# Attention and long convolution on one core: the last product of VectorE's exponential made by GpSimd

## The chip, the cores and the metric

One core of a Trainium2 chip. The metric is the device time of one execution in microseconds (us). The engines are TensorE (PE in the profile; PEld its weight loads), VectorE (DVE), ScalarE (ACT), GpSimd (POOL) and SyncE (SP). GpSimd and SyncE also issue DMA transfers, each from a queue of its own that is worked off in order.

## The reference

Two independent blocks share the program, and their results stand side by side in the output:

```python
def _A_ref(x, wqkv, wo):              # x: 1 x 2048 x 512, 32 heads of 16
    qkv = ((x @ wqkv).reshape(B, S, 3, H, Dh)).transpose(2, 0, 3, 1, 4)
    scores = einsum("bhqd,bhkd->bhqk", q, k) * (Dh ** -0.5)
    p = softmax(scores, axis=-1)
    o = einsum("bhqk,bhkd->bhqd", p, v)
    return o.transpose(0, 2, 1, 3).reshape(B, S, D) @ wo

def _B_ref(q, k, v, shift_k, ssm_k, ssm_D):   # each 1 x 2048 x 512
    kv = shifted_sum(k, shift_k) * v          # 4 taps
    y = causal convolution of kv with ssm_k over 2048 positions, by FFT
    return q * (y + kv * ssm_D)
```

All inputs and the output are bf16. Part A needs 32 x 2048 x 2048 exponentials, and they are most of the work.

## The kernel before, in words

**Blocks.** A block is the scores of one head for 128 keys and 512 queries: one PSUM bank of 128x512 fp32. There are 32 groups (a set of four heads and 512 queries each), 64 blocks to a group, 2048 in all. TensorE makes the scores (`qk_mm`, L810), four heads at once in four row groups of the array.

**Two engines make exponentials.** ScalarE takes two or three blocks at a time (`emit_exp`, L835) from two sets of three PSUM banks and writes them to the ring PT. VectorE takes single blocks (`exp_on_dve`), which TensorE puts into bank BGB or the third bank of a set. [...] L902 reads the scores from PSUM, adds a constant, clips, and stores 16 bits to PTD. The other steps work from SBUF to SBUF on a pair of blocks, 128x1024 elements, in the buffers `low` and `top` of the ring RST: L910 takes the mantissa bits, L914 makes a line of them (fp16), L917 multiplies line and mantissa (the "square"), L920 takes the exponent bits into `low`, and L923 multiplies the square by the number itself into `top` (the "cube", the last product). The block's value is the sum of three terms, PTD, `low` and `top`, and the sum is made by TensorE: the matmul with V (`emit_pv`, L989) accumulates three matmuls for a VectorE block and one for a ScalarE block.

**Order.** The whole program is planned in Python when it is built. Each engine is an `Eng` with a clock `t`; `op(fn, deps, us=...)` appends an instruction, its semaphore waits and its planned end. Each step T of the main loop emits scores and ScalarE's exponentials for some chunk, the matmuls with V of earlier chunks, and background work. Queued VectorE steps stand in `flow`; `pick` and `advance` issue them where the plan says that they can start. `dve_block` decides when VectorE gets a block. In the last stretch of a group it refuses by a fixed number of remaining blocks (GAP). A VectorE pair may begin when the pair three earlier (`R_RST`) has left the ring RST. What is planned becomes a fixed instruction order on each engine; at run time only the semaphores decide.

**Part B.** The convolution is done by TensorE as matmuls of rows of the kernel (WR, streamed by SyncE's queue, L355) with KV (L1215). Results are copied to YB (L1231) and turned back by `conv_turn`: eight matmuls with a permuted identity as the moving operand (L1244), read from IDN with a step of 32 elements; then L1251 multiplies by q in QN. After the eighth turn of a half, QN is stored by GpSimd's queue and reloaded for the second half by `load_qn`, whose first transfer waits for the store. The products kv are made by L573 out of four staged quarters of v; the first three are staged in buffers that are used later for something else, and the fourth in VS2.

**GpSimd before.** It fills constants at the start (L448 to L461), builds a diagonal by an affine select on 128x2048 elements (L629), and otherwise issues DMAs (L355): 120 small ones that spread q into QT, in 15 groups of eight, 15 stores of the attention output, and the loads and stores of QN.

Further line numbers of the trace: L553 moves q out of PSUM, L562 keys, L586 values, L1060 to L1080 end a group (transposes, reciprocal, product), L1142 moves the output rows. After the change the lines have moved: L922, L926, L929 and L932 are what L910, L914, L917 and L920 were, L933 the last product, L914 what L902 was, L819 and L1000 what L810 and L989 were, L844 what L835 was, L1257 the turn.

Of the kernel before, what the change touches and what calls it, by code (L numbers as in the profile page):

```python
# [13 lines left out]
S = 2048  # L14
# [56 lines left out]
MOST_OP = 3  # L71
OVER_OP = 0.1
R_PTD = 5
R_RST = 3
EVEN = 0.85
MOST_D = 3
MORE = 0.1
# [11 lines left out]
MOST = 3  # L89
Q_DUE = 20  # L90
LOOK = 6
GAP = 7
TAIL_GAP = 0
AHEAD = 5
KZ_LATE = 8.0
# [164 lines left out]
def bass_concat_heads__mha_block__ssm_conv_h3__prompt_kernel(  # L260
# [25 lines left out]
    def sb(name, shape, dt=BF16):  # L286
        return enter(nc.sbuf_tensor(name, shape, dt))
# [19 lines left out]
    DTN = sb("DTN", [128, 2, QB])  # L307
    DR = sb("DR", [128, 2, 16], FP32)
    OUTA = sb("OUTA", [128, R_A, D])
    VS2 = sb("VS2", [128, NB * 128])  # L310
    YB = sb("YB", [128, 2, 512])
    IDN = sb("IDN", [128, 128])
    SHK = sb("SHK", [128, 4, 4])
    PTD = sb("PTD", [128, R_PTD, 2, QB])
    RST = sb("RST", [128, R_RST, 2, 2, QB])
# [4 lines left out]
    WV = WKV[:, 0:4 * D].rearrange("p (c f) -> p c f", c=4)  # L320
    WO = WKV[:, 4 * D:8 * D].rearrange("p (o f) -> p o f", o=4)
    VST = [x.rearrange("p (t d) -> p t d", t=NB)
           for x in (WR[:, R_W - 2, 0:S], WR[:, R_W - 1, 0:S], OUTA[:, :, :].rearrange("p r d -> p (r d)"), VS2[:, :])]
# [102 lines left out]
    for c in range(4):  # L426
        for x in range(2):
            src = bass.AP(tensor=v2.tensor, offset=v2[S // 2 * x + 64 * (NB - 1), 128 * c].offset, ap=[[D, 64], [-64 * D, NB], [1, 128]])
            h = dma(sp, d_kv[3 + c], VST[c][x:128:2, :, :], src, kb=256)
        h_vn.append(h)  # L430

    src = bass.AP(tensor=k2.tensor, offset=k2[0:1, 0:1].offset, ap=[[D, S // 2], [S // 2 * D, 2], [1, D]])
    dma(sp, d_kp, kt_ap[LEFT:LEFT + S, :], src, kb=2048)
    dma(sp, d_kp, kt_ap[1:LEFT:2, :], k2[S // 2 - LEFT // 2:S // 2, :], kb=8)
# [14 lines left out]
    for par in range(2):  # L449
# [4 lines left out]
    h_id0 = pool.op(lambda e: e.memset(IDN[:, :], 0.0))  # L454
    h_idn = pool.op(lambda e: e.affine_select(out=IDN[:, :], in_=IDN[:, :], compare_op=ALU.not_equal, fill=1.0,
                                              base=0, pattern=[[-1, 128]], channel_multiplier=1), [h_id0])
    pool.op(lambda e: e.memset(VA[:, :, :, 0:8 * VW].rearrange("p s k (h e) -> p (s k) h e", e=VW)[:, :, :, DH:VW], 1.0))
    h_va1 = pool.op(lambda e: e.memset(VA[:, :, :, 8 * VW:VROW].rearrange("p s k e -> p (s k) e"), 1.0))
    h_kv0 = pool.op(lambda e: e.memset(KV[:, :, NB:2 * NB, :].rearrange("p q w g -> p q (w g)").bitcast(U32), 0), us=(4.4, 4.5))
# [25 lines left out]
    def ready(u):  # L485
        if u[0] == "q":
            return (u[1] < R_Q or 2 * (u[1] - R_Q) + 1 in qk_done) and (u[1] < 2 or 2 * u[1] - 1 in h_q and at(h_q[2 * u[1] - 1]) <= pe.t + 0.5)
        if u[0] == "k":
            return u[1] < 2 or LAST[u[1] - 2] in qk_done
        if u[0] == "v":  # L490
            return u[1] < 2 or LAST[u[1] - 2] in pv_done
        if u[0] == "op":
            return (PAIRS.index((3, u[1])) if u[1] < NQB - 1 else (15, u[2] + 1)) in h_otn and h_wop[0] is not None
        return KT_OF[u[1]][0] in h_kt

    def pe_unit(u, bank, parts=(0, 1, 2, 3)):
        kind = u[0]
# [50 lines left out]
    def evac_unit(u, bank, h):  # L548
        kind = u[0]
        if kind == "q":  # L550
            p = u[1]
            last = [qk_done[2 * (p - R_Q) + i] for i in range(2)] if p >= R_Q else []
            hh = urgent(lambda e: e.tensor_scalar(QS[:, :], PS[:, bank, :], QSCALE, None, ALU.mult),  # L553
                        [h] + [h_q[2 * (p - 1) + i] if p > 1 else None for i in range(2)], us=V512)
            for par in range(2):
                for r0 in range(16 * par, 128, 32):
                    h_q[2 * p + par] = dma(pool, d_qs[p % 2][par], QT[r0:r0 + 16, p % R_Q, par, :], QS[r0:r0 + 16, :],
                                           [hh, h_qt0] + last, kb=16)
        elif kind == "k":
            _, o, sc = u  # L560
            c0 = KEYS0 if (o, sc) == (0, 0) else 0
            hh = urgent(lambda e: e.tensor_copy(KTo[:, o % 2, sc * 512 + c0:(sc + 1) * 512], PS[:, bank, c0:512]),  # L562
                        [h, qk_done[LAST[o - 2]] if o > 1 else None], us=(0.335, 0.46) if c0 else V512)
            h_k[(o, sc)] = hh
            if (o, sc) == (3, 3):
                load_wop(h)
        elif kind == "kv":
            _, c, i = u
            u0 = NB - 4 - 4 * i
            val = VST[c][:, u0:u0 + 4, :].rearrange("p b (q g) -> p b q g", g=4)  # L570
            src = PS[:, bank, :].rearrange("p (b q g) -> p b q g", b=4, g=4)
            dst = KV[:, 32 * c:32 * c + 32, u0:u0 + 4, :].rearrange("p q w g -> p w q g")
            hh = urgent(lambda e: e.tensor_tensor(dst, src, val, ALU.mult), [h, h_vn[c]], us=V512)  # L573
# [132 lines left out]
    def blk(i):  # L706
        return i // (4 * KT), (i // 4) % KT, i % 4
# [11 lines left out]
    def sub(i):  # L719
        n, k, s = blk(i)  # L720
        return n, k // 4 if n == NL else 0
# [173 lines left out]
    def exp_on_dve(b, bank, h):  # L895
# [18 lines left out]
            st["d"] = dve.op(lambda e: e.tensor_scalar(top[:, w].bitcast(FP16), low[:, w], T1, T0, ALU.mult, ALU.add), [st["d"]], us=us)  # L914

        def square(us):
            st["d"] = dve.op(lambda e: e.tensor_tensor(top[:, w].bitcast(FP16), low[:, w], top[:, w].bitcast(FP16), ALU.mult), [st["d"]], us=us)  # L917

        def power(us):
            dve.op(lambda e: e.tensor_scalar(low[:, w].bitcast(U16), lin[:, w].bitcast(U16), 0xFF80, None, ALU.bitwise_and), [st["d"]], us=us)  # L920

        def cube(us):  # L922
            st["d"] = dve.op(lambda e: e.tensor_tensor(top[:, w], top[:, w].bitcast(FP16), lin[:, w], ALU.mult), [st["d"]], us=us)  # L923
# [7 lines left out]
        st["f"][:] = [("p", dep, f, us[n], gate) for f, us, gate in ((mant, FOUR, begin), (line, FOUR, lambda: True), (square, TWO, lambda: True),  # L931
                                                                     (power, FOUR, lambda: True), (cube, TWO, lambda: True))]  # L932

    h_otn = {}
    h_mul = {}
# [236 lines left out]
    def feed_wr(k, h=None):  # L1172
# [6 lines left out]
                wr_next[0] = qd + 1  # L1179
        del wr_todo[:k]  # L1180

    def release():
        h = (pe.sem, pe.n)
        words = BLOCK - pe.at_word % BLOCK
        ends = pe.t + words / (70.0 if busy_conv() else 33.0) + SPAN - LOADED
        while wr_todo and max(dma_t[0], max(at(h) + 0.13, sp.t) + 2.95) + 528 / WR_KB - 0.85 <= ends and pe.t >= pe.crossed + 0.6:
            feed_wr(1, h)
# [46 lines left out]
            state["turn"], state["b"] = True, b  # L1234

    def conv_turn(b, bank):
        own, next_ = [bass.AP(tensor=IDN[:, :].tensor, offset=IDN[0:1, 31:32].offset, ap=[IDN[:, :].ap[0], [-1, n], [32, 4]]) for n in (32, 31)]

        def fn(e):
            ins = None  # L1240
            for k in range(4):
                for part in range(2):
                    y = YB[:, k // 2, 256 * (k % 2) + 128 * part:256 * (k % 2) + 128 * part + 128]
                    ins = e.matmul(PS[:, bank, 128 * k + 4 * part:128 * k + 128], lhsT=y, rhs=(own, next_)[part], start=part == 0, stop=part == 1)  # L1244
            return ins
        h = pe.op(fn, [bank_free[bank], h_ybw[0], h_idn], run=0.445, kind="F")
        h_yb[0] = h
        sl = b // 8
        yv = PS[:, bank, :].rearrange("p (k b g) -> p k b g", k=4, g=4)
# [3 lines left out]
        if b % 8 == 7:  # L1253
# [295 lines left out]
```

## Time and profile before

| what | value |
| --- | --- |
| median of 3 runs | 818.05 us (813.47 to 823.0) |
| the profiled execution | 816.27 us, span 814.5 us |
| ScalarE busy | 777.7 us (95%) |
| VectorE busy | 741.5 us (91%) |
| TensorE busy | 730.1 us (90%), granted clock 0.987 |
| GpSimd busy | 89.9 us (11%) |
| blocks by VectorE / by ScalarE (instruction counts) | 345 / 1703 |

The span goes from the first instruction to the last of the profiled execution; the execution's own time is a little longer. A row of groups reads: line, engine, operation, output <- input, shapes, count | busy us, mean ns of one | idle us of the engine just before them, and who ended it. Busy time counts overlapping instructions once, so a mean duration times a count is more than the busy time. A timeline row reads: start, us, engine, line, operation; several instructions in a row are merged, with their count. A row of waits reads: who waited, for whom, us in total, times, longest. A row of windows gives a stretch, its length, the busy us of PE, PEld, DVE, ACT and POOL, granted clock, DMA share and GB/s.

### The profile page before, as it was taken

How to read it: one execution, taken by the hardware profiler on the slowest of the kernel's cores; microseconds unless marked ns; L12 is line 12 of the kernel's file. 1: busy time of each engine (PE TensorE's matmuls, PEld its weight loads, DVE VectorE, ACT ScalarE, POOL GpSimd, SP SyncE). 2: the span in 40 equal slices, each digit the busy share in tenths (PEclk: the TensorE clock that was granted, in tenths of full speed). 3: DMA queues.
4: the chain of work that ended last, by engine and by line, in shares of the span. 5: the costliest groups of instructions: out<-in, count | busy, mean ns of one | idle time of the engine just before them, and what ended most of it. 6: DMA issues, size and time to landing. Idle time of an engine off the chain costs nothing.

```text
span 814.5 us, 24480 instructions
## 1 busy us (share of the span) xinstructions
PE 730.1 (90%) x10724; PEld 302.5 (37%) x10757; DVE 741.5 (91%) x1480; ACT 777.7 (95%) x633; POOL 89.9 (11%) x160
## 2 busy tenths in 40 slices
PE   7899898989889989999889988989998989898987
PEld 3333343434344333333333333333433423333344
DVE  5799999899989899989999999899999998989985
ACT  7998999999989899999999999999999998999997
POOL 4200230110010102001002400101003020000100
PEclk9999999999989999999999999999999999999999
DMA  9995056577457656677704777586774755664200
GB/s 248 250 282 188 8 125 216 198 252 254 179 184 257 216 215 233 243 271 296 266 2 147 210 277 285 181 327 228 244 274 159 236 207 207 240 234 142 53 2 28
DMA packets 83041, 164.15 MB, mean 202 GB/s; under 512 B 41232, under 2 KB 47256, under 8 KB 82680
## 3 DMA queue, kind: packets, MB, share of 16 engines
q1 hardware_dynamic: 75880, 153.61, 55.3%
q0 software_dynamic: 5856, 8.66, 4.0%
q8 instruction: 85, 1.39, 0.7%
q10 hardware_dynamic: 1200, 0.33, 0.2%
q14 instruction: 20, 0.16, 0.1%
HBM read 149.17 MB, written 8.54 MB: 194 GB/s over the span
## 4 chain that ended last, share of the span: by engine, by line
ACT 49%; DVE 30%; PE 19%; issue 1%
ACT PT L835 49%; DVE PTD L902 9%; PE PS L989 6%; PE PS L810 5%; DVE RST L917 4%; PE PS L1244 4%; DVE RST L923 3%; DVE RST L910 3%; DVE RST L914 3%; DVE RST L920 2%; PE PS L1215 1%; DVE YB L1231 1%; DVE DT L1060 1%; DVE QN L1251 1%; PE PS L526 1%
## 5 line engine op out<-in xcount | busy, mean ns | idle before, releaser
L835 ACT ACTIVATE PT<-PS 128x1536 bf16<-128x1536 f32 (+1 forms) x627 | 774.8, 1386 | 27.8 <-PE PS L810 26.4
L810 PE MATMUL PS<-QT,KTo 32*128 32x512 bf16 (+2 forms) x2248 | 249.8, 368 | 57.8 <-ACT PT L835 23.8
L902 DVE TENSOR_SCALAR PTD<-PS 128x512 uint16<-128x512 f32 x345 | 234.9, 682 | 9.9 <-PE PS L810 9.3
L989 PE MATMUL PS<-PT,VA 128*32 128x512 bf16 (+2 forms) x1873 | 184.1, 372 | 9.4 <-DVE DT L1060 5.0
L810 PEld LDWEIGHTS PS<-QT,KTo 32*128 32x128 bf16 x2248 | 66.8, 91 | 239.3 <-ACT PT L835 154.8
L1413 PE MATMUL PS<-IDN,ZW 128*32 128x512 bf16 (+3 forms) x549 | 126.3, 325 | 0.1
L355 POOL DMA_DIRECT2D QT<-QS x120 | 61.3, 519 | 536.3 <-DVE QS L553 534.1
L917 DVE TENSOR_TENSOR RST<-RST 128x1024 f16<-128x1024 bf16 (+1 forms) x174 | 117.6, 679 | 2.3
L923 DVE TENSOR_TENSOR RST<-RST,PTD 128x1024 bf16<-128x1024 f16 (+1 forms) x174 | 117.3, 674 | 0.0
L1215 PE MATMUL PS<-WR,KV 128*28 128x128 bf16 (+7 forms) x4096 | 90.1, 221 | 1.4 <-issue 0.6
L989 PE MATMUL PS<-RST,VA 128*32 128x512 bf16 (+1 forms) x750 | 90.9, 368 | 0.0
L989 PEld LDWEIGHTS PS<-PT,VA 128*32 128x32 bf16 x1873 | 45.8, 94 | 103.7 <-issue 80.7
L910 DVE TENSOR_SCALAR RST<-PTD 128x1024 uint16<-128x1024 uint16 (+1 forms) x174 | 72.8, 422 | 12.4 <-PE PS L989 11.7
L1215 PEld LDWEIGHTS PS<-WR,KV 128*28 128x28 bf16 (+7 forms) x4096 | 69.1, 102 | 28.0 <-issue 15.9
L914 DVE TENSOR_SCALAR RST<-RST 128x1024 f16<-128x1024 bf16 (+1 forms) x174 | 71.9, 417 | 2.2
L920 DVE TENSOR_SCALAR RST<-PTD 128x1024 uint16<-128x1024 uint16 (+1 forms) x174 | 71.7, 412 | 0.9
L989 PE MATMUL PS<-PTD,VA 128*32 128x512 bf16 (+1 forms) x375 | 67.6, 370 | 0.0
L1413 PEld LDWEIGHTS PS<-IDN,ZW 128*32 128x32 bf16 x549 | 46.0, 96 | 47.6 <-issue 21.1
L989 PEld LDWEIGHTS PS<-RST,VA 128*32 128x32 bf16 x750 | 35.5, 100 | 23.4 <-issue 0.5
L1244 PE MATMUL PS<-IDN,YB 128*128 128x128 bf16 (+1 forms) x128 | 29.9, 388 | 2.1 <-DVE YB L1231 0.9
L1251 DVE TENSOR_TENSOR QN<-PS,QN 128x512 bf16<-128x512 f32 x16 | 11.1, 691 | 19.1 <-PE PS L1244 19.1
L1231 DVE CAST YB<-PS 128x512 bf16<-128x512 f32 x32 | 21.9, 683 | 1.6 <-PE PS L1215 1.3
(74 smaller groups left out, 314.9 us busy)
## 6 DMA issues: line engine op xcount, KB each, us to landing
WR<-kz_scratch SPq DMA_DIRECT2D x256, 528.0 KB, 6.1
kz_scratch<-WR SPq DMA_DIRECT2D x4, 544.0 KB, 6.0
kt_scratch<-in_B_k_dram SPq DMA_DIRECT2D x1, 2048.0 KB
QN<-in_B_q_dram POOLq DMA_DIRECT2D x4, 512.0 KB, 6.7
out_dram<-QN POOLq DMA_DIRECT2D x4, 512.0 KB, 6.3
QT<-QS POOLq DMA_DIRECT2D x120, 16.0 KB, 2.1
out_dram<-OUTA POOLq DMA_DIRECT2D x15, 128.0 KB, 2.2
QN<-in_B_ssm_k_dram SPq DMA_DIRECT2D x1, 1024.0 KB, 8.2
```

The lines of the kernel that those rows point to most:

```text
L810: ins = e.matmul(PS[:, bank, i * w:i * w + w], lhsT=KTo[32 * s:32 * s + 32, OF[n_] % 2, kt * 128:(kt + 1) * 128], rhs=QT[32 * s:32 * s + 3 ...
L835: h_exp[T] = act.op(lambda e: e.activation(PT[:, p0:p0 + n, :].rearrange("p b f -> p (b f)"), PS[:, banks[0]:banks[0] + n, :].rearrange("p ...
L902: st["h"].append(urgent(lambda e: e.tensor_scalar(lin[:, QB * half:QB * half + QB].bitcast(U16), PS[:, bank, :], FIX_ADD, FIX_HI, ALU.add, ...
L910: st["d"] = dve.op(lambda e: e.tensor_scalar(low[:, w].bitcast(U16), lin[:, w].bitcast(U16), 0x7F, 0x3F80, ALU.bitwise_and, ALU.bitwise_or ...
L914: st["d"] = dve.op(lambda e: e.tensor_scalar(top[:, w].bitcast(FP16), low[:, w], T1, T0, ALU.mult, ALU.add), [st["d"]], us=us)
L917: st["d"] = dve.op(lambda e: e.tensor_tensor(top[:, w].bitcast(FP16), low[:, w], top[:, w].bitcast(FP16), ALU.mult), [st["d"]], us=us)
L920: dve.op(lambda e: e.tensor_scalar(low[:, w].bitcast(U16), lin[:, w].bitcast(U16), 0xFF80, None, ALU.bitwise_and), [st["d"]], us=us)
L923: st["d"] = dve.op(lambda e: e.tensor_tensor(top[:, w], top[:, w].bitcast(FP16), lin[:, w], ALU.mult), [st["d"]], us=us)
L989: ins = e.matmul(dst, lhsT=w, rhs=rhs, start=first, stop=last, tile_position=(0, 32 * s))
L1215: ins = e.matmul(dst, lhsT=KV[:, channel(qd) // 4, 2 * n:2 * NB, g], rhs=WR[:, (2 * qd + g // 2) % (R_W), w0:w0 + 128], start=(n == 0), st ...
L1244: ins = e.matmul(PS[:, bank, 128 * k + 4 * part:128 * k + 128], lhsT=y, rhs=(own, next_)[part], start=part == 0, stop=part == 1)
L1413: pe.op(lambda e, s=s, dst=dst, rhs=rhs, rows=rows, first=first: e.matmul(dst, lhsT=ZW[:, 0:rows], rhs=rhs, start=first, stop=first, tile_ ...
```

## The change

1. The last product of a VectorE pair (L923) leaves VectorE. GpSimd makes it, as a tensor_tensor on the same SBUF buffers, as soon as the square is done; the plan gives it 2.8 us for a pair and 1.45 for a single block (`CUBE`). L920 now waits for the square alone. The matmuls with V wait for GpSimd's product and for L920's successor.
2. The ring RST holds four pairs. To make room, VS2 goes: the fourth quarter of v is staged where the third was, and loaded when the third has been used up.
3. `dve_block` no longer uses GAP. It gives VectorE a block while the planned end of VectorE's and GpSimd's queued work (`ends`) lies ahead of ScalarE's planned end for the rest of the group.
4. The turn's permuted identity is copied once at the start by GpSimd into IDP, where it is contiguous; the eight matmuls of a turn read IDP.
5. The reload of QN is put on GpSimd's queue when the plan says that the store has landed, not straight after the store.

The planner makes a new order from this. Counted in the built programs:

| instructions | before | after |
| --- | --- | --- |
| L902 (after: L914), a block taken from PSUM by VectorE | 345 | 383 |
| pairs, 128x1024 / single blocks, 128x512 | 171 / 3 | 191 / 1 |
| last product on VectorE / on GpSimd | 174 / 0 | 0 / 192 |
| ScalarE exponentials on three / two blocks | 449 / 178 | 385 / 255 |
| matmuls in all | 10757 | 10746 |

```diff
-R_RST = 3
+CUBE = {1: (1.45, 1.58), 2: (2.8, 2.93)}
+R_RST = 4
-GAP = 7
+SAFE = 1.5
+RATE = 0.38
+LAST_P = 2.0
...
-    VS2 = sb("VS2", [128, NB * 128])
+    IDP = sb("IDP", [128, 128])
...
+    for c in range(3):
+        load_v(c)
...
+    turned = bass.AP(tensor=IDN[:, :].tensor, offset=IDN[0:1, 31:32].offset, ap=[IDN[:, :].ap[0], [-1, 32], [32, 4]])
+    h_idp = pool.op(lambda e: e.tensor_copy(IDP[:, :].rearrange("p (b g) -> p b g", g=4), turned), [h_idn], us=(0.3, 0.4))
...
+            if c == 2 and kv_n[c] == 4:
+                load_v(3, hh)
...
+    def ends():
+        ahead = [f[0] for f in flow if f and f[0][0] == "p"]
+        t = max(dve.t, pe.t) + sum(us[0] for f in flow for _, _, _, us, _ in f) + V512[0] + LAST_P
+        return max(t, pool.t + CUBE[2][0] * len(ahead)) + CUBE[2][1]
...
-        if left - 3 >= 2.6 * GAP and sub(queue[0]) == x:
-            return pick_row(queue, LOOK)
-        if left - 3 >= 2.6 * GAP:
-            return pick_row(queue[n_act:], 4)
+        if ends() + SAFE <= act.t + RATE * (left - n_act) + 1.3:
+            return pick_row(queue, LOOK) if sub(queue[0]) == x else pick_row(queue[n_act:], 4)
...
         def square(us):
-            st["d"] = dve.op(lambda e: e.tensor_tensor(top[:, w].bitcast(FP16), low[:, w], top[:, w].bitcast(FP16), ALU.mult), [st["d"]], us=us)
+            st["s"] = dve.op(lambda e: e.tensor_tensor(top[:, w].bitcast(FP16), low[:, w], top[:, w].bitcast(FP16), ALU.mult), [st["d"]], us=us)
         def power(us):
-            dve.op(lambda e: e.tensor_scalar(low[:, w].bitcast(U16), lin[:, w].bitcast(U16), 0xFF80, None, ALU.bitwise_and), [st["d"]], us=us)
-
-        def cube(us):
-            st["d"] = dve.op(lambda e: e.tensor_tensor(top[:, w], top[:, w].bitcast(FP16), lin[:, w], ALU.mult), [st["d"]], us=us)
+            st["e"] = dve.op(lambda e: e.tensor_scalar(low[:, w].bitcast(U16), lin[:, w].bitcast(U16), 0xFF80, None, ALU.bitwise_and), [st["s"]], us=us)
+            st["d"] = pool.op(lambda e: e.tensor_tensor(top[:, w], top[:, w].bitcast(FP16), lin[:, w], ALU.mult), [st["s"]], us=CUBE[n])
             for x in st["b"]:
                 h_blk[x] = st["d"]
...
-        deps = [h_blk[b] for b in bl] + [h_v[(OF[blk(b)[0]], kt // 4)] for b in bl for kt, q0, w in tiles(b)]
+        deps = [h_blk[b] for b in bl] + [pairs[on_dve[b][0]]["e"] for b in bl if b in on_dve] + [h_v[(OF[blk(b)[0]], kt // 4)] for b in bl for kt, q0, w in tiles(b)]
...
     def release():
+        if h_out and at(h_out[0]) < pe.t - 1.0:
+            load_qn(1, [h_out.pop()])
...
-                    ins = e.matmul(PS[:, bank, 128 * k + 4 * part:128 * k + 128], lhsT=y, rhs=(own, next_)[part], start=part == 0, stop=part == 1)
+                    ins = e.matmul(PS[:, bank, 128 * k + 4 * part:128 * k + 128], lhsT=y, rhs=IDP[:, 0:128 - 4 * part], start=part == 0, stop=part == 1)
...
             if sl == 0:
-                load_qn(1, [ho])
+                h_out.append(ho)
```

More of the change, by code (lines that the diff above doesn't have):

```diff
@@ L322, in bass_concat_heads__mha_block__ssm_conv_h3__prompt_kernel @@
     VST = [x.rearrange("p (t d) -> p t d", t=NB)
-           for x in (WR[:, R_W - 2, 0:S], WR[:, R_W - 1, 0:S], OUTA[:, :, :].rearrange("p r d -> p (r d)"), VS2[:, :])]
+           for x in (WR[:, R_W - 2, 0:S], WR[:, R_W - 1, 0:S], OUTA[:, :, :].rearrange("p r d -> p (r d)"), OUTA[:, :, :].rearrange("p r d -> p (r d)"))]
     KZS = WRF[:, 0:4 * LKZ].rearrange("p (c m) -> p c m", c=4)
@@ L425, in bass_concat_heads__mha_block__ssm_conv_h3__prompt_kernel, with load_v @@
     h_vn, h_kt = [], {}
-    for c in range(4):
+    def load_v(c, dep=None):
         for x in range(2):
             src = bass.AP(tensor=v2.tensor, offset=v2[S // 2 * x + 64 * (NB - 1), 128 * c].offset, ap=[[D, 64], [-64 * D, NB], [1, 128]])
-            h = dma(sp, d_kv[3 + c], VST[c][x:128:2, :, :], src, kb=256)
+            h = dma(sp, d_kv[3 + c], VST[c][x:128:2, :, :], src, [dep] if x == 0 else (), kb=256)
         h_vn.append(h)
+    for c in range(3):
+        load_v(c)
     src = bass.AP(tensor=k2.tensor, offset=k2[0:1, 0:1].offset, ap=[[D, S // 2], [S // 2 * D, 2], [1, D]])
@@ L493, in ready @@
             return (PAIRS.index((3, u[1])) if u[1] < NQB - 1 else (15, u[2] + 1)) in h_otn and h_wop[0] is not None
-        return KT_OF[u[1]][0] in h_kt
+        return KT_OF[u[1]][0] in h_kt and (u[1] < 3 or len(h_vn) > 3 and at(h_vn[3]) <= pe.t)
     def pe_unit(u, bank, parts=(0, 1, 2, 3)):
@@ L931, in exp_on_dve @@
         st["f"][:] = [("p", dep, f, us[n], gate) for f, us, gate in ((mant, FOUR, begin), (line, FOUR, lambda: True), (square, TWO, lambda: True),
-                                                                     (power, FOUR, lambda: True), (cube, TWO, lambda: True))]
+                                                                     (power, FOUR, lambda: True))]
     h_otn = {}
@@ L1180, in feed_wr @@
         del wr_todo[:k]
+    h_out = []
     def release():
+        if h_out and at(h_out[0]) < pe.t - 1.0:
+            load_qn(1, [h_out.pop()])
         h = (pe.sem, pe.n)
@@ L1236, in conv_turn @@
     def conv_turn(b, bank):
-        own, next_ = [bass.AP(tensor=IDN[:, :].tensor, offset=IDN[0:1, 31:32].offset, ap=[IDN[:, :].ap[0], [-1, n], [32, 4]]) for n in (32, 31)]
         def fn(e):
@@ L1243, in fn @@
                     y = YB[:, k // 2, 256 * (k % 2) + 128 * part:256 * (k % 2) + 128 * part + 128]
-                    ins = e.matmul(PS[:, bank, 128 * k + 4 * part:128 * k + 128], lhsT=y, rhs=(own, next_)[part], start=part == 0, stop=part == 1)
+                    ins = e.matmul(PS[:, bank, 128 * k + 4 * part:128 * k + 128], lhsT=y, rhs=IDP[:, 0:128 - 4 * part], start=part == 0, stop=part == 1)
             return ins
-        h = pe.op(fn, [bank_free[bank], h_ybw[0], h_idn], run=0.445, kind="F")
+        h = pe.op(fn, [bank_free[bank], h_ybw[0], h_idp], run=0.445, kind="F")
         h_yb[0] = h
```

## The prediction

> **What bounds the kernel now.** I read the page first: the busy times, the chain that ended last, the costliest groups.
>
> ```profile
> span 814.5 us, 24480 instructions
> ...
> PE 730.1 (90%) x10724; PEld 302.5 (37%) x10757; DVE 741.5 (91%) x1480; ACT 777.7 (95%) x633; POOL 89.9 (11%) x160
> ...
> ACT 49%; DVE 30%; PE 19%; issue 1%
> ...
> L835 ACT ACTIVATE PT<-PS 128x1536 bf16<-128x1536 f32 (+1 forms) x627 | 774.8, 1386 | 27.8 <-PE PS L810 26.4
> ...
> L902 DVE TENSOR_SCALAR PTD<-PS 128x512 uint16<-128x512 f32 x345 | 234.9, 682 | 9.9 <-PE PS L810 9.3
> ...
> L355 POOL DMA_DIRECT2D QT<-QS x120 | 61.3, 519 | 536.3 <-DVE QS L553 534.1
> L917 DVE TENSOR_TENSOR RST<-RST 128x1024 f16<-128x1024 bf16 (+1 forms) x174 | 117.6, 679 | 2.3
> L923 DVE TENSOR_TENSOR RST<-RST,PTD 128x1024 bf16<-128x1024 f16 (+1 forms) x174 | 117.3, 674 | 0.0
> ...
> L910 DVE TENSOR_SCALAR RST<-PTD 128x1024 uint16<-128x1024 uint16 (+1 forms) x174 | 72.8, 422 | 12.4 <-PE PS L989 11.7
> ```
>
> ScalarE's exponential (L835) is busy 774.8 us and waits 27.8 in all, so ScalarE is the bound; VectorE, at 741.5 with its own exponential, is 36 us behind it. GpSimd looks idle (11%). The profiled execution took 816.27 us (span 814.5, 1.8 around it); the median shown is 818.05, 0.2% above. Sums go against 816.27. About 1% is what a measurement of this kernel can tell from no change.
>
> Then the groups with shapes kept apart, for what one block costs ScalarE:
>
> ```profile
> L835 ACT ACTIVATE PT<-PS 128x1536 bf16<-128x1536 f32 x449 | 625.4, 1507 | 14.4 <-PE PS L810 13.5
> L835 ACT ACTIVATE PT<-PS 128x1024 bf16<-128x1024 f32 x178 | 185.5, 1081 | 13.4 <-PE PS L810 12.9
> ```
>
> One block of 512 columns is 1507-1081 = 0.426 us. Next the timeline of VectorE, for what an instruction really occupies: durations overlap their successors, so I take the step by which a second one in a merged row lengthens it, or the next start.
>
> ```profile
> 46.84 0.75 DVE L910 TENSOR_SCALAR RST<-PTD 128x1024 uint16<-128x1024 uint16 x2
> ...
> 48.78 1.28 DVE L917 TENSOR_TENSOR RST<-RST 128x1024 f16<-128x1024 bf16 x2
> ...
> 53.05 0.68 DVE L923 TENSOR_TENSOR RST<-RST,PTD 128x1024 bf16<-128x1024 f16 x1
> 53.65 0.68 DVE L902 TENSOR_SCALAR PTD<-PS 128x512 uint16<-128x512 f32 x1
> ```
>
> L910 (and L914, L920, of the same size) occupies 0.33 us, L917 and L923 0.60, and L902 0.60 (its 0.68 less the same overlap). A pair costs 2x0.60 + 3x0.33 + 2x0.60 = 3.4 us.
>
> **The row that decides.** GpSimd does almost no arithmetic in this trace, but once, at its start, it does so beside VectorE:
>
> ```profile
> 14.81 2.01 POOL L629 TENSOR_SCALAR_AFFINE_SELECT OTN<-SHK 128x2048 bf16<-128x2048 bf16 x1 [5.95 <-DMA SHK<-in_B_shift_k_dram]
> ```
> ```profile
> 14.02 1.48 DVE L902 TENSOR_SCALAR PTD<-PS 128x512 uint16<-128x512 f32 x2
> 15.54 1.56 DVE L910 TENSOR_SCALAR RST<-PTD 128x1024 uint16<-128x1024 uint16 x1
> 17.14 0.43 DVE L914 TENSOR_SCALAR RST<-RST 128x1024 f16<-128x1024 bf16 x1
> ```
>
> GpSimd works from 14.81 to 16.82. L910, issued at 15.54, takes 1.56 us in place of 0.42 and ends at 17.10, 0.28 after GpSimd: about its own length, begun when GpSimd was done. L914 just behind it takes 0.43 again. The two L902, which read PSUM, lose at most 0.2 in the same stretch (1.48 against 1.28). [...]
>
> ```profile
> 761.45 2.23 POOL L355 DMA_DIRECT2D out_dram<-QN  x2 [28.00 <-DVE QN L1251]
> ```
> ```profile
> 762.03 0.77 DVE L914 TENSOR_SCALAR RST<-RST 128x1024 f16<-128x1024 bf16 x1
> ```
>
> So I take it that a SBUF-to-SBUF instruction of VectorE stands still while a GpSimd instruction on SBUF runs. One full example is thin, and of another GpSimd operation; the chances say so. [...]
>
> **The change part by part.** Counts are from the built instruction orders of both kernels.
>
> ScalarE: the new planner gives VectorE 383 blocks for 345. ScalarE loses 38x0.426 = 16.2 us and gains 13 instructions (640 for 627); one has 1507-3x426 = 229 ns beside its blocks, at most 3 us in all, of which I take 1, since durations overlap. Net -15.
>
> VectorE's own work: L923 goes, 171x0.60 + 3x0.33 = -103.6. 38 more L902 at 0.60 = +22.8. 191 whole pairs for 171, at 3x0.33+0.60 = 1.6: +32, less 2 half pairs at about 1: +30. 741.5 - 103.6 + 22.8 + 30 = 690.7 us.
>
> GpSimd: 192 products, 191 of 128x1024. No row shows one. Lower bound from L629: 2048 elements of one input in 2.01 us, and the product reads 2x1024. Upper bound: the 2.8 us that the diff plans for it (CUBE). The plan's figures for GpSimd do not all fit the chip: it has 3.0 for L629 (2.01 above) and 4.4 for L459:
>
> ```profile
> L459 POOL MEMSET KV<- 128x4096 uint32 x1 | 3.5, 3507 | 0.0
> ```
>
> So I stay nearer to L629 than to the plan: 2.3 us. [...]
>
> The stall: a product starts when its square (L929 after the change) is done and VectorE leaves SBUF. VectorE goes on with what reads PSUM until its next SBUF-to-SBUF instruction. In the changed order, 91 of 192 squares have no such instruction behind them, 58 one, 32 two, 11 three to five: 159 in all, at 0.60 us = 0.50 us a square. For the 91 the next L932 runs first, and a mean of 0.93 instructions (0.55 us) follows it: 91/192x0.55 = 0.26. At most 0.76 us is hidden; GpSimd starts some 0.1 late, so 0.6. A product costs VectorE 2.3-0.6 = 1.7 us where it had cost 0.60: 192x1.7 = 326 us, added to 690.7 = 1017.
>
> The new wait: the matmuls with V of a VectorE block (L1000) now wait for GpSimd's product and for L932, where one wait for L923 did. Queued behind a waiting matmul on TensorE are the next scores (L819), for which ScalarE and L914 wait. With VectorE the bound, that wait is where ScalarE's lost time will show; it adds nothing to the sum, since the product's time is in it already, except by the idle time kept below.
>
> What VectorE then idles: 814.5-741.5 = 73 us now.
>
> ```profile
> 0.00:15.00 15.00, 13.04 (x110) 5.66 (x111) 5.98 (x15) 10.04 (x11) 8.10 (x16) 1.00 0.96 195
> ...
> 790.00:814.50 24.50, 19.51 (x503) 13.17 (x507) 13.54 (x37) 17.98 (x17) 1.67 (x3) 0.92 0.07 24
> ```
>
> VectorE is busy 5.98 of the first 15 us and 13.54 of the last 24.5: 20 us of start and tail stay. Of the other 53, waits for slower engines, I keep half, 26, since VectorE is now what others wait for, but blocks have one PSUM bank and a late product holds back TensorE. 1017+46+1.8 = **1065 us**.
>
> The turn's identity (conv_turn):
>
> ```profile
> 188.28 1.87 PE L1244 MATMUL PS<-IDN,YB 128*128 128x128 bf16 x8
> ```
> ```profile
> 186.73 0.75 PE L1215 MATMUL PS<-WR,KV 128*20 128x128 bf16 x40
> ```
> ```profile
> DVE QN L1251 <- PE PS L1244: 19.1, 16, 1.6
> ```
>
> Eight strided matmuls take 1.87 us; 40 contiguous ones of 128 columns 0.75, so eight take about 0.4 to 0.6. 16 turns save TensorE about 20 us, and VectorE most of the 19.1 it waits for them; that lies in the idle time that I halved. While ScalarE is the bound, ScalarE's 27.8 us of waits is a ceiling for it; at 188.28 it is 0.46 (row under the rivals), so 16x0.4 = 6.
>
> The ring of four removes at most the waits before L910 (12.4 us in all, 11.7 of them for TensorE, first fence); I give it nothing, since the stall delays VectorE by more. The last quarter of v is now loaded when the third has been used, and the copy for the new identity is added at the start:
>
> ```profile
> VS<-in_B_v_dram SPq DMA_DIRECT2D x2, 256.0 KB, 5.9
> ```
> ```profile
> L573 DVE TENSOR_TENSOR KV<-PS,VS x4: 681/688/692, 240.6 to 321.5; 128x512 bf16<-128x512 f32 x4
> L573 DVE TENSOR_TENSOR KV<-PS,OUTA x2: 680/682/685, 142.3 to 162.6; 128x512 bf16<-128x512 f32 x2
> ```
> ```profile
> L455 POOL TENSOR_SCALAR_AFFINE_SELECT IDN<-IDN 128x128 bf16<-128x128 bf16 x1 | 0.3, 283 | 0.2 <-POOL IDN L454 0.2
> ```
>
> The third quarter is used up at 162.6 and the fourth first wanted at 240.6: 78 us for two issues that land in 5.9, with kernel-row loads ahead of and behind them on SP's queue; if that queue is held up, one late unit waits some 6 us. A 128x128 piece costs GpSimd 0.28 us before anything waits for it. The reload of QN, now queued after its store has landed rather than in front of other work, takes a wait off GpSimd's queue. All three: 0. GpSimd's queue is in order: 120 QT issues of 0.519 (L355) stand in 15 groups of eight, and a product behind one is 4.2 us late. If each held VectorE or TensorE back, 15x4.2 = 63; the ring of four covers one pair (3 us) of it, and I add none to the sum.
>
> **The rivals.** *No exclusion for this product* (other side). GpSimd works beside VectorE as the plan has it. For it: GpSimd is 11% busy, 192x2.3 = 442 us fits; against it: the 1.56 row. ScalarE stays the bound: 816.3-15-6 = **795 us**.
>
> ```profile
> 190.51 9.75 ACT L835 ACTIVATE PT<-PS 128x1024 bf16<-128x1024 f32 x8 [0.46 <-PE PS L810]
> ```
>
> Where it turns: 690.7 + 46 + 1.8 + 192x0.4 = 815, so VectorE reaches the old time when a product stops it for 0.4 us, or, with 0.6 hidden, when it shuts VectorE out for 1.0, half of the lower bound.
>
> *GpSimd yields*: it waits for VectorE, and VectorE seldom for it. Then port time adds up, without other loss: 192x(1.6+2.3) = 749, QT issues 61, 20 of start and tail, 20 of poor fit: **850 us**. Nothing in the trace shows VectorE going first.
>
> *The gain is lost to lateness*: no exclusion, but products behind eight QT issues, or taking 2.8, hold TensorE back by as much as ScalarE saves: 15x1.4 = 21 against -21, **816 us**.
>
> **Chances.** Exclusion with VectorE as bound 0.70; no exclusion 0.17; GpSimd yields 0.10; lateness 0.03. Faster by over 1%: 0.17; within: 0.03; slower: 0.80. Within the first case, the low end has a product of 2.0 with all 0.76 hidden and 20 idle: 690.7+238+20+2 = 951; the high end 2.8 with 0.4 hidden and all 73 idle: 690.7+461+73+2 = 1227. Taking in the yielding case, the range is 845 to 1230; 0.2 is left out below it.
>
> **What would show it.** The exclusion: L922, L926, L929 and L932 with durations far above 0.42 and 0.68 while L914 keeps 0.68; VectorE near 1020 us busy, ScalarE below 80%, ScalarE's waits for TensorE, and TensorE's for L914, far longer. The counts: 640 exponentials with about 760 us busy. The product: L933 at 2.0 to 2.8 us. The turn: L1257 below 250 ns. I am wrong if L922 and L932 keep 0.42 with L933 running, or if L933 itself stretches while VectorE does not.

## The result, and the profile after

The changed kernel takes 1034.45 us (median of 4 runs, 1031.11 to 1036.56) against 815.92 us for the kernel before (4 runs): a ratio of 1.266, 95% interval 1.257 to 1.275. Its profiled execution took 1036.56 us, span 1034.8.

The page of the changed kernel: busy times, the chain that ended last, and the groups that answer to those shown before.

```profile
span 1034.8 us, 24654 instructions
...
PE 783.7 (76%) x10710; PEld 315.2 (30%) x10746; DVE 940.5 (91%) x1416; ACT 783.6 (76%) x646; POOL 516.5 (50%) x353
...
DVE 72%; PE 21%; issue 4%; ACT 3%; DVEq 0%
...
L844 ACT ACTIVATE PT<-PS 128x1536 bf16<-128x1536 f32 (+1 forms) x640 | 780.7, 1287 | 241.9 <-PE PS L819 239.3
L933 POOL TENSOR_TENSOR RST<-RST,PTD 128x1024 bf16<-128x1024 f16 x192 | 425.2, 2216 | 429.7 <-DVE RST L929 429.4
...
L914 DVE TENSOR_SCALAR PTD<-PS 128x512 uint16<-128x512 f32 x383 | 258.0, 680 | 14.7 <-PE PS L819 13.8
...
L932 DVE TENSOR_SCALAR RST<-PTD 128x1024 uint16<-128x1024 uint16 x192 | 208.1, 1084 | 2.9
...
L922 DVE TENSOR_SCALAR RST<-PTD 128x1024 uint16<-128x1024 uint16 x192 | 135.9, 714 | 28.3 <-PE PS L1000 27.9
L929 DVE TENSOR_TENSOR RST<-RST 128x1024 f16<-128x1024 bf16 x192 | 148.9, 776 | 1.3
L926 DVE TENSOR_SCALAR RST<-RST 128x1024 f16<-128x1024 bf16 x192 | 126.7, 664 | 1.2
```

VectorE has lost 174 products and is busy 199 us longer (940.5 for 741.5). The chain, 49% ScalarE before, is now 72% VectorE, and ScalarE waits 241.9 us for 27.8. L932 has a mean of 1084 ns; before, as L920, it had 414:

```profile
L920 DVE TENSOR_SCALAR RST<-PTD 128x1024 uint16<-128x1024 uint16 x171 | 70.8, 414 | 0.9
```

L922 and L926 rise to 714 and 664 and the square L929 to 776. L914, which reads PSUM, keeps 680 ns. GpSimd is busy half of the time, so its queue is not too full.

The timelines of GpSimd and of VectorE in one stretch (start, us, engine, line) show how it comes about:

```profile
302.82 2.37 POOL L933 TENSOR_TENSOR RST<-RST,PTD 128x1024 bf16<-128x1024 f16 x1 [3.78 <-DVE RST L929]
307.08 2.37 POOL L933 TENSOR_TENSOR RST<-RST,PTD 128x1024 bf16<-128x1024 f16 x1 [1.90 <-DVE RST L929]
310.54 2.12 POOL L933 TENSOR_TENSOR RST<-RST,PTD 128x1024 bf16<-128x1024 f16 x1 [1.09 <-DVE RST L929]
```
```profile
302.06 0.68 DVE L929 TENSOR_TENSOR RST<-RST 128x1024 f16<-128x1024 bf16 x1
302.78 0.43 DVE L932 TENSOR_SCALAR RST<-PTD 128x1024 uint16<-128x1024 uint16 x1
303.12 2.35 DVE L926 TENSOR_SCALAR RST<-RST 128x1024 f16<-128x1024 bf16 x1
305.39 0.41 DVE L922 TENSOR_SCALAR RST<-PTD 128x1024 uint16<-128x1024 uint16 x1
...
310.38 0.68 DVE L914 TENSOR_SCALAR PTD<-PS 128x512 uint16<-128x512 f32 x1
310.98 1.96 DVE L932 TENSOR_SCALAR RST<-PTD 128x1024 uint16<-128x1024 uint16 x1
```

The product at 302.82 finds VectorE on SBUF with L932, is recorded from there and takes 2.37 us; the one at 310.54 starts beside L914, which reads PSUM, and takes 2.12. The first ends at 305.19 and L926, recorded from 303.12, at 305.47; the third at 312.66 and L932 at 312.94. Counted over the whole trace: 156 of these VectorE instructions (37 L922, 26 L926, 5 L929, 88 L932) begin inside a product with more than 0.1 us of it left, and every one ends 0.28 to 0.29 us after it (L929 0.55 to 0.56), about its own length. Of 80 L914 that begin so, none takes over 0.69 us.

### The profile page after: what moved, and what is told of

Same layout as the page of the kernel before. It is cut to its first block, busy times and chain, and to the rows that moved or that the text cites. A ratio compares the mean times of both kernels' runs of the same rounds, so it can differ in the third digit from the quotient of the medians.

```text
span 1034.8 us, 24654 instructions
## 1 busy us (share of the span) xinstructions
PE 783.7 (76%) x10710; PEld 315.2 (30%) x10746; DVE 940.5 (91%) x1416; ACT 783.6 (76%) x646; POOL 516.5 (50%) x353
## 4 chain that ended last, share of the span: by engine, by line
DVE 72%; PE 21%; issue 4%; ACT 3%; DVEq 0%
DVE PTD L914 18%; DVE RST L932 14%; DVE RST L929 11%; DVE RST L922 10%; DVE RST L926 9%; PE PS L1000 8%; PE PS L819 6%; ACT PT L844 3%; PE PS L1426 2%; DVE DT L1071 2%; PE PS L1230 1%; DVE YB L1246 1%; DVE VA L595 1%; DVE OUTA L1153 1%; DVE DTN L1082 1%
## 5 line engine op out<-in xcount | busy, mean ns | idle before, releaser
L844 ACT ACTIVATE PT<-PS 128x1536 bf16<-128x1536 f32 (+1 forms) x640 | 780.7, 1287 | 241.9 <-PE PS L819 239.3
L933 POOL TENSOR_TENSOR RST<-RST,PTD 128x1024 bf16<-128x1024 f16 x192 | 425.2, 2216 | 429.7 <-DVE RST L929 429.4
L819 PE MATMUL PS<-QT,KTo 32*128 32x512 bf16 (+2 forms) x2248 | 274.7, 400 | 169.2 <-DVE PTD L914 106.6
L914 DVE TENSOR_SCALAR PTD<-PS 128x512 uint16<-128x512 f32 x383 | 258.0, 680 | 14.7 <-PE PS L819 13.8
L932 DVE TENSOR_SCALAR RST<-PTD 128x1024 uint16<-128x1024 uint16 x192 | 208.1, 1084 | 2.9
L922 DVE TENSOR_SCALAR RST<-PTD 128x1024 uint16<-128x1024 uint16 x192 | 135.9, 714 | 28.3 <-PE PS L1000 27.9
L929 DVE TENSOR_TENSOR RST<-RST 128x1024 f16<-128x1024 bf16 x192 | 148.9, 776 | 1.3
L926 DVE TENSOR_SCALAR RST<-RST 128x1024 f16<-128x1024 bf16 x192 | 126.7, 664 | 1.2
L1000 PE MATMUL PS<-RST,VA 128*32 128x512 bf16 (+1 forms) x850 | 120.2, 416 | 0.0
L1230 PE MATMUL PS<-WR,KV 128*30 128x128 bf16 (+7 forms) x4096 | 99.4, 231 | 7.0 <-DVE PTD L914 4.3
L1230 PEld LDWEIGHTS PS<-WR,KV 128*30 128x30 bf16 (+7 forms) x4096 | 74.7, 106 | 40.1 <-issue 20.7
L1000 PEld LDWEIGHTS PS<-PTD,VA 128*32 128x32 bf16 x425 | 23.1, 105 | 9.0 <-issue 4.5
```

Source lines behind the costliest of these rows:

```text
L819: ins = e.matmul(PS[:, bank, i * w:i * w + w], lhsT=KTo[32 * s:32 * s + 32, OF[n_] % 2, kt * 128:(kt + 1) * 128], rhs=QT[32 * s:32 * s + 3 ...
L844: h_exp[T] = act.op(lambda e: e.activation(PT[:, p0:p0 + n, :].rearrange("p b f -> p (b f)"), PS[:, banks[0]:banks[0] + n, :].rearrange("p ...
L914: st["h"].append(urgent(lambda e: e.tensor_scalar(lin[:, QB * half:QB * half + QB].bitcast(U16), PS[:, bank, :], FIX_ADD, FIX_HI, ALU.add, ...
L922: st["d"] = dve.op(lambda e: e.tensor_scalar(low[:, w].bitcast(U16), lin[:, w].bitcast(U16), 0x7F, 0x3F80, ALU.bitwise_and, ALU.bitwise_or ...
L929: st["s"] = dve.op(lambda e: e.tensor_tensor(top[:, w].bitcast(FP16), low[:, w], top[:, w].bitcast(FP16), ALU.mult), [st["d"]], us=us)
L932: st["e"] = dve.op(lambda e: e.tensor_scalar(low[:, w].bitcast(U16), lin[:, w].bitcast(U16), 0xFF80, None, ALU.bitwise_and), [st["s"]], us=us)
```

## The experiments

The theory: a GpSimd instruction that reads and writes SBUF shuts VectorE's SBUF-to-SBUF steps out for its length (exclusion). The rival, called lateness below: the loss comes from the long way of the product through GpSimd's queue, the waits on it, and the new order.

**A product that nobody waits for.** In the kernel before, one line is added behind the square, and a private buffer filled with ones:

```diff
+            h_spr[0] = pool.op(lambda e: e.tensor_tensor(SPR[:, 0:448 * n], SPR[:, 0:448 * n], SPR[:, 0:448 * n], ALU.mult), [st["d"], h_spr[0]], us=(0.0, 0.0))
```

> The kernel before, with one thing added: after each square GpSimd multiplies a private buffer of 896 (for single blocks 448) elements a partition by itself. Nobody waits for it, and the orders of the other four engines are those of before. Exclusion theory: each of the 174 idle products, about 1.9 us long, stops VectorE's SBUF-to-SBUF instructions for about 1.1 us (2.2 us gave some 1.3 after the change), of which VectorE's idle time takes up some 30 us in all: 816+174*1.1-30 = 977, range 940 to 1020, with L913, L917, L920, L923 and L926 (the SBUF steps) drawn out and L905 (from PSUM) not. Rival, lateness (the loss comes from waiting for GpSimd's product and from the new order): nobody waits and the order is old, so 816, range 808 to 830, with all VectorE durations as before.

In its trace the steps are L912, L916, L919, L923 and L926, and L904 is the one from PSUM. Measured: 990.09 us, ratio 1.213 (1.210 to 1.216). Busy times and groups of VectorE, then GpSimd's product:

```profile
PE 795.1 (80%) x10724; PEld 318.2 (32%) x10757; DVE 906.3 (92%) x1480; ACT 795.4 (80%) x633; POOL 393.4 (40%) x335
...
L904 DVE TENSOR_SCALAR PTD<-PS 128x512 uint16<-128x512 f32 x345 | 234.7, 681 | 21.7 <-PE PS L812 21.5
L923 DVE TENSOR_SCALAR RST<-PTD 128x1024 uint16<-128x1024 uint16 x171 | 180.5, 1055 | 0.9
L926 DVE TENSOR_TENSOR RST<-RST,PTD 128x1024 bf16<-128x1024 f16 x171 | 155.9, 911 | 0.0
```
```profile
L920 POOL TENSOR_TENSOR SPR<-SPR 128x896 bf16<-128x896 bf16 (+1 forms) x174 | 303.5, 1744 | 519.9 <-DVE RST L919 518.6
```

Nothing depends on this product and VectorE's order is unchanged, yet the kernel is 174 us slower, and the first SBUF step after the square, L923, goes from 414 to 1055 ns. Lateness cannot do this. VectorE's busy time is 906.3 us, 164.8 more than before, so 164.8/174 = 0.95 us are lost to a product of 1.74.

**A fill in its place.** The added line is a memset of the same 896 elements, which reads nothing:

```diff
+            h_spr[0] = pool.op(lambda e: e.memset(SPR[:, 0:448 * n], 1.0), [st["d"], h_spr[0]], us=(0.0, 0.0))
```

> The same, but GpSimd only fills the private buffer (a memset of 896 elements, about 0.8 us, that reads nothing). If any GpSimd instruction on SBUF excludes VectorE's SBUF steps: about 0.4 us each, 174*0.4-30 = 40, so 855, range 830 to 890, with the square drawn out as well. If only what is shared counts (a write against the three 4-wide steps, not against the two products, which need the second read): about half of that, 825 to 850, with L920 and L926 at 0.68. Rival, lateness: 816, range 808 to 826.

Measured: 869.52 us, ratio 1.064 (1.061 to 1.068).

```profile
L923 DVE TENSOR_SCALAR RST<-PTD 128x1024 uint16<-128x1024 uint16 x171 | 123.2, 720 | 0.9
L919 DVE TENSOR_TENSOR RST<-RST 128x1024 f16<-128x1024 bf16 x171 | 116.3, 683 | 2.2
L926 DVE TENSOR_TENSOR RST<-RST,PTD 128x1024 bf16<-128x1024 f16 x171 | 115.2, 673 | 0.0
```
```profile
L920 POOL MEMSET SPR<- 128x896 bf16 (+1 forms) x174 | 152.7, 878 | 541.0 <-DVE RST L919 539.9
```

A write alone stops L923 (720 ns). The time came out at the size expected for general exclusion, above the 825 to 850 of the narrower one, but the products keep 683 and 673 ns, as expected for the narrower one. L923 stands first behind the fill, so hardly any product began inside one: four L926 and one L919 did, and took 0.67 to 0.69 us. The next run has more of them.

**The fill behind the exponent step.** The same memset waits for the step that takes the exponent bits, so the next thing on VectorE is often the last product:

```diff
-            dve.op(lambda e: e.tensor_scalar(low[:, w].bitcast(U16), lin[:, w].bitcast(U16), 0xFF80, None, ALU.bitwise_and), [st["d"]], us=us)
+            h_e = dve.op(lambda e: e.tensor_scalar(low[:, w].bitcast(U16), lin[:, w].bitcast(U16), 0xFF80, None, ALU.bitwise_and), [st["d"]], us=us)
+            h_spr[0] = pool.op(lambda e: e.memset(SPR[:, 0:448 * n], 1.0), [h_e, h_spr[0]], us=(0.0, 0.0))
```

> The kernel before with a memset of a private buffer by GpSimd (896 elements) that waits for the step that takes the exponent bits and so starts beside VectorE's last product, which reads two SBUF operands two at a time. If a GpSimd instruction that only writes excludes that one too, either the fill is stretched from 0.88 to some 1.4 us or the product from 0.68 to 1.4. If it excludes only the 4-wide steps, the last product keeps 0.68 with a fill of 0.88 inside, and the loss is less than the 53 us of the fill behind the square: 820 to 860.

Measured, one execution: 826.18 us.

```profile
303.54 0.68 DVE L926 TENSOR_TENSOR RST<-RST,PTD 128x1024 bf16<-128x1024 f16 x1
```
```profile
303.68 0.84 POOL L923 MEMSET SPR<- 128x896 bf16 x1 [3.86 <-DVE RST L922]
```

The two run beside each other at full length. An L912 that begins inside a fill does not:

```profile
328.43 0.86 POOL L923 MEMSET SPR<- 128x896 bf16 x1
```
```profile
328.51 1.07 DVE L912 TENSOR_SCALAR RST<-PTD 128x1024 uint16<-128x1024 uint16 x1
```

Over the whole trace, 33 last products and five squares begin inside a fill, and none takes over 0.69 us. With more than 0.1 us of a fill left, 22 L912, 11 L916 and one L922 begin, and all end 0.28 us after it. So in these runs a fill excludes the one-input steps on bits and line (34 of them here on L912, L916 and L922; L923 at 720 ns in the run before) and not the products with two inputs (33 and five at no more than 0.69 us), and a product on GpSimd excludes both kinds (five L929 of up to 2.62 us in the changed kernel; L926 with a mean of 911 ns in the first run, for 679 before). What the expectations call 4-wide, and two at a time for the product, is relative: in the kernel before, 512 elements more cost a one-input step 0.13 us (L914, 420 for 294 ns) and a product 0.26 (L917, 683 for 425), 0.25 and 0.50 ns an element, against 1.02 for a transpose out of PSUM (L1060 and L1094, 708 for 512 elements, 315 for 128). What a fill shares with the one kind and not with the other, no run shows.

**No product, the order of the change.** GpSimd's product is cut to two elements a partition and stays in every queue and wait:

```diff
-            st["d"] = pool.op(lambda e: e.tensor_tensor(top[:, w], top[:, w].bitcast(FP16), lin[:, w], ALU.mult), [st["s"]], us=CUBE[n])
+            st["d"] = pool.op(lambda e: e.tensor_tensor(top[:, 0:2], top[:, 0:2].bitcast(FP16), lin[:, 0:2], ALU.mult), [st["s"]], us=CUBE[n])
```

> The changed kernel with its order on VectorE, TensorE and ScalarE as it is; GpSimd's product is cut to 2 of the 1024 (or 512) elements a partition, so that nearly all of the product is left out and its place in all queues and waits stays. Exclusion theory: without time on SBUF there is no stall; VectorE has 690 us of work, ScalarE is the bound with 38 blocks less than before, so the time is that of the identity alone less 15: 797-15 = 782, range 772 to 797; L922, L926, L932 back near 420 ns, L929 near 680. Rival, lateness (order, queues of GpSimd, later waits of TensorE): the loss stays, 950 or more.

Measured: 783.97 us, ratio 0.960 (0.957 to 0.964), as expected. The page's busy times, and groups of VectorE:

```profile
PE 703.0 (90%) x10746; PEld 290.1 (37%) x10746; DVE 692.6 (88%) x1416; ACT 759.1 (97%) x646; POOL 150.8 (19%) x353
```
```profile
L929 DVE TENSOR_TENSOR RST<-RST 128x1024 f16<-128x1024 bf16 x191 | 130.2, 681 | 1.2
L932 DVE TENSOR_SCALAR RST<-PTD 128x1024 uint16<-128x1024 uint16 x191 | 80.6, 422 | 2.9
```

The instructions and order on VectorE are those of the change; only the length of GpSimd's product differs. The difference of VectorE's busy times, 940.5-692.6 = 247.9 us, is therefore what 192 products cost it: 1.29 us each. The order, the queues and the eight QT issues ahead of a product cost nothing that shows. A product of two elements is also done early, so what a late product makes others wait for is not in this run; but the spans differ by 1034.8-782.9 = 251.9 us, and VectorE's busy time is 247.9 of that. Only 4 us are left for such waits and for the lower TensorE clock (0.881 granted, for 0.998) together. The plan's gain is there, and exclusion eats it.

**Half of the product.** As above, with 512 elements (`QB`) for every product.

```diff
+            st["d"] = pool.op(lambda e: e.tensor_tensor(top[:, 0:QB], top[:, 0:QB].bitcast(FP16), lin[:, 0:QB], ALU.mult), [st["s"]], us=CUBE[n])
```

> The changed kernel, the product cut to 512 elements a partition also for whole pairs (half of the product is left out); orders of VectorE, TensorE and ScalarE as in the change. Exclusion theory: a product of 1.1 to 1.25 us, of which the same 0.8 as after the change is hidden, so 0.4 of stall for 1.3: VectorE 690+192*0.4 = 767 busy and some 50 to 70 idle: 830, range 805 to 870. If nothing were hidden and the loss went in step with the length, half of 1035-782: 908. Rival, lateness: 1030.

Measured: 856.52 us, ratio 1.049 (1.045 to 1.053).

```profile
PE 722.9 (85%) x10746; PEld 300.0 (35%) x10746; DVE 775.5 (91%) x1416; ACT 769.6 (90%) x646; POOL 334.6 (39%) x353
...
L933 POOL TENSOR_TENSOR RST<-RST,PTD 128x512 bf16<-128x512 f16 x192 | 241.5, 1259 | 432.3 <-DVE RST L929 431.9
```

The stall is (775.5-692.6)/192 = 0.43 us. The 1259 ns are a mean with drawn-out products in it (those that begin beside L932 take up to 1.41 us); one that begins beside L914 takes 1.16 us, where the whole product takes 2.12. So 1.16-0.43 = 0.73 us of the half product is hidden and 2.12-1.29 = 0.83 of the whole one, nearly the same, and 0.96 us more of GpSimd's work costs VectorE 0.86 us more.

**Every fourth pair.** GpSimd makes the product of pairs 0, 4, 8 and so on, VectorE the others.

```diff
+        def cube(us):
+            eng = dve if j % 4 else pool
+            st["d"] = eng.op(lambda e: e.tensor_tensor(top[:, w], top[:, w].bitcast(FP16), lin[:, w], ALU.mult), [st["s"]], us=us)
```

> The changed kernel with the product on GpSimd for every fourth pair only (46 pairs by the plan, 137 on VectorE, 363 blocks on VectorE in all). Exclusion theory: each GpSimd product stops VectorE for 1.3 us and saves it 0.6, so VectorE's work is that of the kernel with all products on it plus about 46*0.7 = 32, plus 20 blocks' share: slower than the 799 with all products on VectorE, 830, range 812 to 865. Rival, lateness by a queue that is too full: with a quarter of the products the queue is nearly empty and the gain of the 18 to 20 blocks that ScalarE loses shows: 790 to 798.

Measured: 857.09 us, ratio 1.049 (1.045 to 1.053). VectorE is busy 811.8 us:

```profile
PE 722.0 (84%) x10734; PEld 296.1 (35%) x10734; DVE 811.8 (95%) x1497; ACT 777.0 (91%) x636; POOL 193.0 (23%) x207
...
L938 POOL TENSOR_TENSOR RST<-RST,PTD 128x1024 bf16<-128x1024 f16 x46 | 101.0, 2196 | 431.2 <-DVE RST L929 431.1
```

This is slower than with all products on VectorE (799.31, below). The direction is that of exclusion; the time is 27 us above the expectation, within its range. VectorE is the bound here: 79% of the chain, and its 811.8 us with 43.2 idle are the span of 855.0. It is busy 58.9 us more than with all products on it (752.9), but it also has 20 blocks more (363 for 343), since the plan saw room for them. How much of the loss each of the two makes was not tested.

**The product back on VectorE, all else of the change.**

```diff
-            st["d"] = pool.op(lambda e: e.tensor_tensor(top[:, w], top[:, w].bitcast(FP16), lin[:, w], ALU.mult), [st["s"]], us=CUBE[n])
+        def cube(us):
+            st["d"] = dve.op(lambda e: e.tensor_tensor(top[:, w], top[:, w].bitcast(FP16), lin[:, w], ALU.mult), [st["e"]], us=us)
...
-        return max(t, pool.t + CUBE[2][0] * len(ahead)) + CUBE[2][1]
+        return t
```

> All of the change except that VectorE makes the last product again: ring of four, contiguous identity, later loads, the new rule for the end of a group (343 blocks on VectorE by the plan, 345 before). Exclusion theory: with no GpSimd product the stall is gone, and what is left is identity and ring: 808, range 798 to 816. Rival, lateness by the new order and queues: the loss of the other parts stays, 850 or more.

Measured: 799.31 us, ratio 0.980 (0.977 to 0.982), at the low end of the expected range.

```profile
PE 708.7 (89%) x10699; PEld 294.7 (37%) x10736; DVE 752.9 (94%) x1473; ACT 775.2 (97%) x638; POOL 91.2 (11%) x161
```

**The identity alone**, in the kernel before: IDP is added and the turn reads it.

```diff
-                    ins = e.matmul(PS[:, bank, 128 * k + 4 * part:128 * k + 128], lhsT=y, rhs=(own, next_)[part], start=part == 0, stop=part == 1)
+                    ins = e.matmul(PS[:, bank, 128 * k + 4 * part:128 * k + 128], lhsT=y, rhs=IDP[:, 0:128 - 4 * part], start=part == 0, stop=part == 1)
```

> The kernel before with the contiguous identity for the turn and nothing else of the change; the other engines' orders are as before. Both theories: eight matmuls of a turn take 0.4 to 0.7 us for 1.87; ScalarE stays the bound and loses 16*0.4 = 6 us of waits: 810, range 804 to 814. VectorE's waits for the turn fall from 19.1 to about 4.

Measured: 796.66 us, ratio 0.977 (0.975 to 0.979), the fastest of the kernels here that compute the whole result. The gain is 19.6 us where 6 were expected, and the time lies below the expected range. Busy times, a group of TensorE and the waits of ScalarE; then both rows as they were before:

```profile
PE 707.1 (89%) x10724; PEld 295.8 (37%) x10757; DVE 741.6 (93%) x1480; ACT 773.8 (97%) x633; POOL 90.4 (11%) x161
```
```profile
L1245 PE MATMUL PS<-IDP,YB 128*128 128x128 bf16 x64 | 9.0, 222 | 2.3 <-DVE YB L1234 1.1 <-DVE PTD L905 0.9
```
```profile
ACT PT L838 <- PE PS L813: 11.5, 26, 1.0
```
```profile
L1244 PE MATMUL PS<-IDN,YB 128*128 128x128 bf16 x64 | 24.9, 389 | 2.1 <-DVE YB L1231 0.9 <-DVE PTD L902 0.8
```
```profile
ACT PT L835 <- PE PS L810: 26.4, 51, 1.7
```

The matmuls of a turn take 222 ns for 389. ScalarE's waits for scores fall from 26.4 to 11.5 us. From the timelines of ScalarE: within 8 us after the start of a turn it waited some 14 us in all before and 1 us now. Half of the 14 is the wait right behind the turn (0.20 to 0.84 each, 7.1 together); half came some microseconds later, I think because TensorE was still behind.

Against this, the kernel with all other parts but GpSimd's product (799.31) is no faster: ring, later loads and the new end rule together gain nothing. They were not tried one by one.

## Why the prediction was right, point by point

The forecast was 1065 us and the direction slower; measured 1034. The mechanism, exclusion of VectorE's SBUF steps by GpSimd, was read from one row of 1.56 us, and held in 156 cases. The size is right in part by luck: two terms were mis-sized in opposite directions, the stall 79 us too large and VectorE's idle time 48 us too small, and so the sum is only 31 us too high. The range, 845 to 1230, was wide.

- *The product's time and what is hidden of it.* Predicted 2.3 us with 0.6 hidden, a stall of 1.7; measured 2.12 undisturbed, 0.83 hidden, 1.29. L629 came nearer: 2.01 us for as many reads. GpSimd began 0.08 us after the square (302.82, the square's end at 302.74), where I took 0.1. The plan's 2.8 was too long. 192x0.41 = 79 us too much: VectorE is busy 940.5 us where I had 1017.
- *VectorE's own work.* Predicted 690.7; 692.6 without the stall.
- *VectorE's idle time.* I kept half of 53 us of waits, 46 us in all with start and tail. It is 1034.8-940.5 = 94 us, 48 more. Waits of the changed kernel:

```profile
PE PS L819 <- DVE PTD L914: 106.6, 92, 4.1
DVE RST L922 <- PE PS L1000: 27.9, 20, 4.0
DVE YB L1246 <- PE PS L1230: 15.8, 7, 5.0
```

  The same waits with the two-element product:

```profile
DVE RST L922 <- PE PS L1000: 33.3, 28, 4.7
DVE YB L1246 <- PE PS L1230: 12.8, 8, 3.9
PE PS L819 <- DVE PTD L914: 4.2, 13, 0.6
```

  TensorE's waits for VectorE to free a bank grow with the stall: 4.2 us, 35.8 with half of the product, 106.6 with the whole. VectorE's waits for the matmuls with V, to free a pair of the ring, do not, in spite of the fourth pair: 33.3, 26.5 and 27.9 us. They mostly stand before the same pairs in all three kernels. One of the longest, before the 123rd L922, is 4.7, 3.5 and 4.0 us. So I read them as coming with the order that the plan made for the change and not with the stall (with two elements VectorE also has time to spare, so this is not a clean test); half of what the old order waited was the wrong measure. The kernel with every fourth pair, which VectorE bounds too but which has another order, idles 43.2 us, and its L922 waits 1.4. What in the order of the change makes the waits stays open.
- *ScalarE.* -15 us: ScalarE is busy 759.1 without the stall, against 773.8 with the identity alone, -14.7. In the changed kernel it is 783.6, and the exponentials 780.7, not the some 760 that I named as a sign: busy time counts overlaps once, and activations that wait overlap less (640 of a mean 1287 ns, 824 us in all; without the stall 640 of 1364, 873 us in all, are busy 756.1). The no-exclusion rival, 795, would have been 784; what it missed is the next point.
- *The identity.* Predicted 6 us while ScalarE is the bound; it gave 19.6. I took one wait right behind a turn times 16, and left out the waits of ScalarE some microseconds later. Eight matmuls of a turn take 0.61 us, at the upper end of my 0.4 to 0.6. In the changed kernel one takes 260 ns, a little over the 250 that I named, at a granted clock of 0.881; with the identity alone it is 222 at 0.996.
- *The duration of L914, and no full queue on GpSimd.* As said: 680 ns, and POOL at 50%.
- *The row that decides.* What I took from it is too wide: a fill does not stop the two-input products, and some SBUF-to-SBUF steps run on beside a product (last section). That the square stands still too was an estimate: the trace of before has no square beside GpSimd's arithmetic, and the changed kernel has five, of 2.40 to 2.62 us. The DMA issue at 761.45, with L914 beside it at 0.77 us, bears it out less than I took it to. Beside the issues of the kernel before, only three one-input steps are drawn out clearly (0.53, 0.57 and 0.77 us), and beside the 120 issues to QT none takes over 0.47 us.
- *The other rivals.* Yielding: VectorE waited for GpSimd in 156 cases; GpSimd's product was stretched too, but only by the one instruction that was running (2.37 for 2.12). No run shows a port, on whose time the 850 us were added up, an estimate of mine; what the runs show is that the 156 instructions ended 0.28 to 0.56 us after the product. Lateness: excluded by the product that nobody waits for, and by VectorE's busy time against the run with two elements.

## What to carry to other kernels

Before work goes from VectorE to an idle GpSimd, look at how VectorE's steps read and write. Here most are SBUF to SBUF, and each product that moved cost VectorE its length on GpSimd less what was hidden of it, 2.12-0.83 = 1.29 us, for a saving of 0.60; GpSimd's busy share of 11% before said nothing about it. One stretched row in a trace, two engines beside each other, can be read as such an exclusion if the end of the one gives the end of the other; how far it reaches, here not to every operation, took runs of its own. An operand with a step in a small matmul, sixteen times in a program, was worth more (19.6 us) than the shift of work would have been without the stall (796.66-783.97 = 12.7 us), and half of the waits behind it came some microseconds later, not in the next row.

## What the runs showed of the hardware

- What a GpSimd instruction stopped differed between a product, which reads and writes SBUF, and a fill, which only writes. In the changed kernel the product stopped the one-input steps L922, L926 and L932 (151 cases, up to 2.36 us for 0.42) and the square L929 (five cases, up to 2.62 us for 0.68); the one that nobody waits for also drew out the last product (a mean of 911 ns for 679). The fill stopped one-input steps (34 cases behind the exponent step; L923 at 720 ns for 414 behind the square) and no product (33 last products and five squares, none over 0.69 us). Steps from PSUM (80 L914 that began inside a product, at most 0.69 us), and transposes from SBUF to SBUF (L1091, 0.70 us for 4 that began inside a product), ran on.
- GpSimd's product of 1024 bf16 and fp16 elements took 2.12 us undisturbed, 2.1 ns an element.
- A moving operand read with a step of 32 elements took 389 ns for a 128-column matmul (granted clock 0.987), contiguous 222 (0.996).
- The granted TensorE clock was lower in the runs in which TensorE was busy for a smaller share of the span and its scores waited longer for VectorE's reads of PSUM: 0.987 before (busy 90%, 15.2 us of such waits), 0.881 after the change (76%, 106.6), 0.907 with the product that nobody waits for (80%, 83.3), 0.998 with the two-element one (90%, 4.2). Which of the two follows from the other was not tested.
